# Token halves of 512 and 448 instead of 502 and 500 in a chain of attention and two feed-forward layers

## The chip, the cores and the metric

The kernel runs on one core of a Trainium2 chip. The metric is device time in microseconds (us) of one execution, given as the median of several runs. The engines are TensorE (PE in the profile, with PEld for its weight loads), VectorE (DVE), ScalarE (ACT), GpSimd (POOL) and SyncE (SP, which here issues every DMA).

## What is computed

The reference, cut to what matters (6016 tokens, 256 channels, 2048 hidden units, all float32):

```python
qn = q / (np.linalg.norm(q, axis=1, keepdims=True) + 1e-06)
kn = k / (np.linalg.norm(k, axis=1, keepdims=True) + 1e-06)
s = kn.transpose(0, 2, 1) @ qn / tau          # 256 x 256, channels by channels
a = softmax(s, axis=-1)
x = (v @ a).reshape(6016, 256)
h = x @ moe_w_in                               # 256 -> 2048
x = (h * np.clip(h + 3.0, 0.0, 6.0) / 6.0) @ moe_w_out
h = x @ moe2_w_in
out = np.maximum(h, 0.0) ** 2 @ moe2_w_out
```

## The kernel before, in words

**Start.** Scores are summed over 47 blocks of 128 tokens (`score`, L293, plain float32 matmuls of 256 columns) while q and k stream in, the squares of q and k are summed on ACT and DVE (`squares`, L288), and the 256 x 256 softmax follows. The softmax matrix is multiplied into the first layer's weights (the `m1_*` functions, L440 to L489, matmuls of 512 columns), so that v needs no product of its own.

**Pieces.** The tokens are cut into six pieces, and each piece into two halves of equal width (`WIDTHS`, L24: four pieces of halves of 502 tokens, two of 500; `WMAX` = 502 is the row length of nearly every tile). Tokens lie along the free axis, so a half's width is the number of columns of a matmul. Layer j (0 or 1) treats pieces p = 0 to 5 one after the other, so the kernel works through twelve pairs (j, p).

**High and low parts.** Every float32 operand x is kept as hi (x rounded to float32r, made by a copy on ACT) and lo (x minus hi, made by a subtraction on DVE or POOL); `split`, L115. `passes` (L298) makes one product of three matmuls: L304 multiplies the weights' hi with the tokens' hi, L305 the weights' lo with the tokens' hi, L306 the weights' hi with the tokens' lo. So L306 is the one that streams a lo row. Tokens' hi and lo are the two rows of one tile `[P, 2, WMAX]` (`operand` L495, `g_tile` L578): the lo row begins WMAX numbers behind the hi row.

**The first pair, (0, 0),** is done plainly: 32 steps (`first`, `product`, `second`, L596 to L618) of 12 matmuls each, 384 in all, while the first layer's weights are still being converted.

**The other eleven pairs** go through `strassen` (L702): 8 units to a pair, a unit being a 2 x 2 block product of 7 products in place of 8 (`mult`, targets `x`, `y`, `q`) and 8 products with the second weights (`group`, L551, target `acc`). That makes 15 products, 45 matmuls, to a unit and 360 to a pair. A unit also has 3 copies out of PSUM on ACT (L726), 3 additions on DVE (L730), the activation (L736, L738 on ACT; L744, L749 on DVE), and a hi copy and a lo subtraction for each of four blocks (L753 on ACT, L120 on DVE).

**Order.** It is written by hand: `at(place, ...)` (L643) puts a step at a place, `run` plays the steps in the order of their places, 15 places to a unit. `prepare` (L651) loads the next pair's tokens three and a half units ahead and makes its operands on POOL and ACT (L670 to L685). `second_in` and `second_out` (L212, L249) convert the second layer's weights on ACT, DVE and POOL in the time of pairs (0, 1) to (0, 4). Each pair's result is copied out of PSUM (`evict`, L560) and stored to DRAM, at last to `out`.

**Small tiles.** `ident` and `ones` (L104, L106) lie in the pool `const`. `small(n)` (L270) hands out pieces of four `scratch` tiles of 2 x WMAX numbers, the first tile with room taken first.

Of the kernel before, what the change touches and what calls it, by code (L numbers as in the profile page):

```python
# [8 lines left out]
F32 = mybir.dt.float32  # L9
# [7 lines left out]
P = 128  # L17
# [3 lines left out]
NT = NTOK // P  # L21
KC = C // P
KF = DFF // P
WIDTHS = [502] * 4 + [500] * 2  # L24
NP = len(WIDTHS)
WMAX = max(WIDTHS)
NU = KF // 2
# [23 lines left out]
def attention_then_two_ffns(  # L51
# [32 lines left out]
    const = ctx.enter_context(tc.tile_pool(name="const", bufs=1))  # L84
# [3 lines left out]
    ops = ctx.enter_context(tc.tile_pool(name="ops", bufs=1))  # L88
# [12 lines left out]
        return ps_h.tile(shape, F32, tag=tag, name=name, bufs=2 if tag == "y" else 1)  # L101


    ident = const.tile([P, P], F32, name="ident")  # L104
    make_identity(nc, ident)
    ones = const.tile([P, P], F32, name="ones")  # L106
    nc.gpsimd.memset(ones, 1.0)
    three = const.tile([P, 1], F32, name="three")
    nc.gpsimd.memset(three, 3.0)
# [198 lines left out]
    with tc.manual_schedule():  # L308
# [50 lines left out]
        def load_x(j, p, raw):  # L359

            w = WIDTHS[p]
            for k in range(KC):
# [132 lines left out]
        def operand(j, p, r):  # L495
# [6 lines left out]
            else:  # L502
                t = ops.tile([P, 2, WMAX], F32R, tag=f"op{r}", name=f"x{j}_{p}_{r}")
            t = t[:, :, :WIDTHS[p]]
            operands[j, p, r] = [t[:, i, :] for i in range(2)]
# [5 lines left out]
        def split_first(k):  # L511
            w = WIDTHS[0]
            for n in range(2):
                hi, lo = x0[k, n] = operand(0, 0, ((B11, T3), (B21, B22))[k][n])
                split(hi, lo, raw0[k][:, n, :w])
# [35 lines left out]
        def group(j, p, u, f, n, d, gs, first, last):  # L551

            w = WIDTHS[p]
            if first:
# [355 lines left out]
```

## Time and profile before

| what | value |
|---|---|
| median of 3 runs | 1092.11 us (1091.79 to 1092.32) |
| profiled execution, its own time | 1092.65 us |
| its span, first to last instruction | 1090.9 us |
| PE busy | 1068.3 us, 98% |
| DVE busy | 864.4 us, 79% |
| ACT busy | 675.0 us, 62% |
| POOL busy | 246.3 us, 23% |
| mean granted TensorE clock | 0.993 |

The span starts with the first instruction, and all places in the trace are counted from there. Matmuls overlap: a matmul's recorded length runs from its entering the array to its last result, so the pace of TensorE is read from the distance between the starts of two matmuls, not from their lengths.

### The profile page before, as it was taken

The numbers are of one execution on the slowest core, as the hardware profiler recorded it, in microseconds if no ns is written. First come the engines' busy times: TensorE is split into PE (matmuls) and PEld (weight loads), VectorE is DVE, ScalarE is ACT, GpSimd is POOL, SyncE is SP. The second block draws the span as 40 slices with busy tenths as digits, with TensorE's granted clock in tenths as the row PEclk, the third lists the DMA queues.
The fourth block names the chain that finished last, engine by engine and source line by source line (L and its number), as shares of the span: only waits on it lengthen the run. The fifth ranks groups of instructions, "written<-read, shape, count | busy, mean of one in ns | idle before, by whom it ended". The sixth has DMA issues, their size and how long they took to land.

```text
span 1090.9 us, 13113 instructions
## 1 busy us (share of the span) xinstructions
PE 1068.3 (98%) x4630; PEld 873.8 (80%) x4630; DVE 864.4 (79%) x1283; ACT 675.0 (62%) x1196; POOL 246.3 (23%) x215
## 2 busy tenths in 40 slices
PE   9989899999999999999999999999999999999998
PEld 7868677878878877788888888888888888888886
DVE  6798977888888888888678778778778778778765
ACT  6677667778677767777666455445445445445443
POOL 0022351162342154043013003003003003003000
PEclk9999999999999999999999999999999999999999
DMA  9721302213312311410254100100100100100001
GB/s 348 297 63 34 96 1 78 91 56 113 129 53 77 130 53 51 156 54 28 116 192 175 65 1 29 48 1 29 48 1 23 54 1 10 67 0 16 23 1 38
DMA packets 26451, 77.66 MB, mean 71 GB/s; under 512 B 2833, under 2 KB 11025, under 8 KB 26385
## 3 DMA queue, kind: packets, MB, share of 16 engines
q1 hardware_dynamic: 26384, 76.82, 19.5%
q8 instruction: 36, 0.59, 0.2%
q14 instruction: 31, 0.25, 0.1%
HBM read 52.95 MB, written 23.86 MB: 70 GB/s over the span
## 4 chain that ended last, share of the span: by engine, by line
PE 79%; DVE 10%; issue 4%; ACT 4%; POOL 2%; DMA 1%; SPq 0%; DVEq 0%; POOLq 0%; ACTq 0%
PE acc L306 13%; PE acc L304 13%; PE acc L305 13%; PE y L304 7%; PE y L306 6%; PE y L305 6%; PE q L304 3%; PE s L294 3%; PE q L306 3%; PE q L305 3%; DVE gs L120 3%; DVE g L744 2%; DVE h L730 2%; PE x L304 2%; PE x L306 2%
## 5 line engine op out<-in xcount | busy, mean ns | idle before, releaser
L120 DVE TENSOR_TENSOR gs<-g,gs 128x502 fp32r<-128x502 f32 (+1 forms) x384 | 282.9, 755 | 64.9 <-ACT gs L753 58.9
L306 PE MATMUL acc<-gs,wo 128*128 128x502 f32 (+1 forms) x768 | 302.5, 394 | 0.5 <-DVE gs L120 0.5
L305 PE MATMUL acc<-gs,wo 128*128 128x502 f32 (+1 forms) x768 | 300.7, 392 | 1.1 <-DVE wo L120 1.1
L304 PE MATMUL acc<-gs,wo 128*128 128x502 f32 (+1 forms) x768 | 301.5, 393 | 0.1
L753 ACT CAST gs<-g 128x502 fp32r<-128x502 f32 (+1 forms) x352 | 214.7, 612 | 107.6 <-DVE g L749 54.4
L306 PEld LDWEIGHTS acc<-gs,wo 128*128 128x128 f32 x768 | 146.1, 190 | 32.7 <-DVE gs L120 2.5
L304 PEld LDWEIGHTS acc<-gs,wo 128*128 128x128 f32 x768 | 146.7, 191 | 31.0 <-ACT gs L118 0.8
L305 PEld LDWEIGHTS acc<-gs,wo 128*128 128x128 f32 x768 | 145.7, 190 | 31.5 <-DVE wo L120 1.4
L685 POOL TENSOR_TENSOR x<-raw,x 128x502 fp32r<-128x502 f32 (+1 forms) x55 | 72.8, 1331 | 333.0 <-ACT x L681 332.8
L749 DVE SCALAR_TENSOR_TENSOR g<-h 128x502 f32<-128x502 f32 (+1 forms) x144 | 120.4, 836 | 3.1
L744 DVE SCALAR_TENSOR_TENSOR g<-r,h 128x502 f32<-128x502 f32 (+1 forms) x120 | 97.4, 812 | 29.1 <-ACT r L736 25.2
L736 ACT ACTIVATE r<-h,three 128x502 f32<-128x502 f32 (+1 forms) x120 | 85.9, 716 | 32.5 <-DVE h L730 32.2
L730 DVE TENSOR_TENSOR h<-q,su 128x502 f32<-128x502 f32 (+1 forms) x88 | 59.6, 678 | 48.9 <-PE q L306 48.2
L730 DVE TENSOR_TENSOR h<-q,se 128x502 f32<-128x502 f32 (+1 forms) x88 | 59.7, 678 | 35.9 <-ACT se L726 35.6
L738 ACT ACTIVATE r<-y 128x502 f32<-128x502 f32 (+1 forms) x48 | 28.3, 590 | 88.4 <-PE y L306 88.4
L726 ACT COPY se<-y 128x502 f32<-128x502 f32 (+1 forms) x88 | 50.7, 576 | 41.6 <-PE y L306 41.0
L726 ACT COPY su<-y 128x502 f32<-128x502 f32 (+1 forms) x88 | 50.1, 569 | 34.9 <-PE y L306 34.9
L726 ACT COPY sa<-y 128x502 f32<-128x502 f32 (+1 forms) x88 | 50.2, 571 | 33.5 <-PE y L306 33.1
L730 DVE TENSOR_TENSOR h<-x,sa 128x502 f32<-128x502 f32 (+1 forms) x88 | 59.5, 676 | 10.5 <-PE x L306 9.8
L294 PE MATMUL s<-qk 128*128 128x256 f32 x188 | 43.3, 391 | 0.8 <-DMA qk<-in_qk 0.8
L294 PEld LDWEIGHTS s<-qk 128*128 128x128 f32 x188 | 36.6, 197 | 6.6 <-DMA qk<-in_qk 1.6
L670 POOL TENSOR_TENSOR t<-raw 128x502 f32<-128x502 f32 (+1 forms) x11 | 14.6, 1328 | 112.6 <-DMA raw<-x2d 112.6
(240 smaller groups left out, 1883.9 us busy)
## 6 DMA issues: line engine op xcount, KB each, us to landing
qk<-in_qk SPq DMA_DIRECT2D x23, 512.0 KB, 7.4
wo<-in_w_out SPq DMA_DIRECT2D x16, 512.0 KB, 4.4
wi<-in_w_in SPq DMA_DIRECT2D x10, 512.0 KB, 4.2
wo2d<-wo2s SPq DMA_DIRECT2D x8, 512.0 KB, 3.0
wo<-wo2d SPq DMA_DIRECT2D x8, 512.0 KB, 3.5
x2d<-o SPq DMA_DIRECT2D x16, 251.0 KB, 2.3
raw<-x2d SPq DMA_DIRECT2D x8, 502.0 KB, 4.8
out<-o SPq DMA_DIRECT2D x16, 251.0 KB, 2.3
```

The lines of the kernel that those rows point to most:

```text
L120: (rest or nc.vector).tensor_tensor(out=lo, in0=x, in1=f32(hi), op=ALU.subtract)
L294: nc.tensor.matmul(s_ps[i], lhsT=x[:, C + i * P:C + (i + 1) * P], rhs=x[:, :C], start=(t == 0), stop=(t == NT - 1))
L304: nc.tensor.matmul(ps, lhsT=ah, rhs=bh, start=first, stop=False, skip_group_check=more)
L305: nc.tensor.matmul(ps, lhsT=al, rhs=bh, start=False, stop=False, skip_group_check=more)
L306: nc.tensor.matmul(ps, lhsT=ah, rhs=bl, start=False, stop=last, skip_group_check=more)
L685: nc.gpsimd.tensor_tensor(out=l, in0=ts[r], in1=f32(h), op=ALU.subtract)
L726: nc.scalar.copy(s[tag], s["y"])
L730: nc.vector.tensor_tensor(out=s[which], in0=s[ps], in1=s[tag], op=ALU.add)
L736: nc.scalar.activation(s["r" + which], h, AF.Relu, bias=three)
L744: nc.vector.scalar_tensor_tensor(out=g, in0=s["r" + which], scalar=6.0, in1=h, op0=ALU.min, op1=ALU.mult)
L749: nc.vector.scalar_tensor_tensor(out=g, in0=h, scalar=0.0, in1=r, op0=ALU.max, op1=ALU.mult)
L753: nc.scalar.copy(gs[which][0], s["g" + which])
```

## The change

Only widths, row lengths and the places of a few small tiles change.

```diff
-WIDTHS = [502] * 4 + [500] * 2
+WIDTHS = [512] * 5 + [448]
...
-    ident = const.tile([P, P], F32, name="ident")
+    both = ops.tile([P, 512], F32, tag="t0", name="both")
+    ident, ones = both[:, :P], both[:, P:2 * P]
     make_identity(nc, ident)
-    ones = const.tile([P, P], F32, name="ones")
     nc.gpsimd.memset(ones, 1.0)
```

`WMAX` follows and becomes 512, so every operand tile is `[P, 2, 512]`: the lo row begins 512 numbers behind the hi row, where it began 502 behind. The halves add up to 3008 tokens in either case. `both` takes a buffer (`t0`) that `prepare` uses later for the sums of the tokens' blocks; that frees the room of `ident` and `ones` in the pool `const`. The scratch tiles grow from 1004 to 1024 numbers, and so `small` packs its pieces otherwise: both sums of squares now lie in the first tile, and the fourth stays empty.

On every engine the same instructions stand in the same order as before, and all but one wait are for the same count of the same engine. The one is on ACT, at the copies of the first product's results (`m`, L472, and the first activation, L607): a wait for POOL stands three instructions earlier (`mp` are that product's PSUM tiles, `rs` the softmax's row sums, L464 the hi copies of the new weights). Before:

```order
L464 ACTIVATE a_0_533<-mp_0_501,rs_495 128x256 [waits DVE_49]
L464 ACTIVATE wa_0h<-mp_1_538,rs_509 128x2x256 [waits PE_49]
L472 ACTIVATE m_0_0_547<-mp_0_501,rs_495 128x512 [waits DVE_49]
L472 ACTIVATE m_0_1_549<-mp_1_538,rs_509 128x512 [waits DVE_49]
L152 ACTIVATE tywo_0_529<-wo_0_431 128x512
L607 ACTIVATE r_0_0_579<-h_0_0_565,three 128x502 [waits PE_49,Pool_49]
```

And with the change:

```order
L464 ACTIVATE a_0_532<-mp_0_500,rs_494 128x256 [waits DVE_49]
L464 ACTIVATE wa_0h<-mp_1_537,rs_508 128x2x256 [waits PE_49]
L472 ACTIVATE m_0_0_546<-mp_0_500,rs_494 128x512 [waits DVE_49,Pool_49]
L472 ACTIVATE m_0_1_548<-mp_1_537,rs_508 128x512 [waits DVE_49]
L152 ACTIVATE tywo_0_528<-wo_0_430 128x512
L607 ACTIVATE r_0_0_578<-h_0_0_564,three 128x512 [waits PE_49]
```

What moved is the wait for POOL alone; the width of the activation shows the new half.

## Rows read from the trace of the kernel before

**Rows 1.** The page: busy time of each engine, and the span in 40 slices.

```profile
PE 1068.3 (98%) x4630; PEld 873.8 (80%) x4630; DVE 864.4 (79%) x1283; ACT 675.0 (62%) x1196; POOL 246.3 (23%) x215
...
PE   9989899999999999999999999999999999999998
...
POOL 0022351162342154043013003003003003003000
```

**Rows 2.** Windows by pair: busy us (count) of each engine, granted clock, DMA share, GB/s.

```profile
165.00:249.00 84.00, 81.83 (x349) 64.95 (x349) 68.43 (x102) 63.22 (x113) 27.45 (x27) 1.00 0.22 79
249.00:337.00 88.00, 85.40 (x363) 69.23 (x363) 74.66 (x111) 65.63 (x119) 29.01 (x28) 0.98 0.25 89
337.00:423.00 86.00, 83.03 (x361) 67.40 (x360) 73.39 (x108) 64.63 (x117) 30.28 (x28) 1.00 0.24 86
423.00:507.00 84.00, 83.19 (x364) 67.71 (x363) 70.45 (x106) 63.99 (x116) 29.39 (x28) 1.00 0.22 78
507.00:588.00 81.00, 80.99 (x358) 67.01 (x357) 60.60 (x90) 55.80 (x97) 13.93 (x11) 1.00 0.35 133
...
753.00:835.00 82.00, 82.00 (x361) 67.84 (x360) 63.46 (x91) 40.88 (x73) 14.97 (x11) 1.00 0.07 26
```

**Rows 3.** Timeline of PE: first matmuls of the last pairs' first units (start, length).

```profile
670.68 0.39 PE L304 MATMUL y<-x,wa_0h 128*128 128x502 f32 x1
...
752.92 0.39 PE L304 MATMUL y<-x,wa_0h 128*128 128x502 f32 x1
...
835.22 0.39 PE L304 MATMUL y<-x,wa_0h 128*128 128x502 f32 x1
...
917.58 0.39 PE L304 MATMUL y<-x,wa_0h 128*128 128x500 f32 x1
...
999.39 0.40 PE L304 MATMUL y<-x,wa_0h 128*128 128x500 f32 x1
...
1060.63 0.40 PE L304 MATMUL y<-x,wa_3h 128*128 128x500 f32 x1
```

**Rows 4.** Timeline of PE: matmuls of 512 columns, and the short ones after them.

```profile
54.05 0.39 PE L306 MATMUL mp<-wi1l,eth 128*128 128x512 f32 x1
...
54.97 0.83 PE L280 MATMUL busy<-ones 128*128 128x128 f32 x6
...
106.00 0.40 PE L304 MATMUL mp<-wi1h,eth 128*128 128x512 f32 x1
...
106.93 0.40 PE L305 MATMUL mp<-wi1h,etl 128*128 128x512 f32 x1
```

**Rows 5.** Timeline around the stall at 317 us: PE, ACT.

```profile
317.20 0.39 PE L306 MATMUL acc<-gs,wo 128*128 128x502 f32 x1
...
317.64 0.62 ACT L235 CAST wa2s<-w 128x512 fp32r<-128x512 f32 x1 [1.45 <-POOL w L210]
...
319.90 0.49 PE L304 MATMUL y<-x,wa_3h 128*128 128x502 f32 x1 [2.31 <-ACT su L726]
...
321.51 0.62 PE L304 MATMUL acc<-gs,wo 128*128 128x502 f32 x1
...
321.93 0.62 PE L305 MATMUL acc<-gs,wo 128*128 128x502 f32 x1
```

**Rows 6.** Lines by form (busy us, mean ns): POOL's lo, and DVE additions from PSUM.

```profile
L685 POOL TENSOR_TENSOR x<-raw,x 128x502 fp32r<-128x502 f32 x35 | 46.0, 1322 | 212.1 <-ACT x L681 212.0
...
L730 DVE TENSOR_TENSOR h<-q,se 128x502 f32<-128x502 f32 x56 | 38.0, 678 | 20.2 <-ACT se L726 19.9
...
L291 DVE TENSOR_TENSOR scratch<-sq,scratch 128x512 f32<-128x512 f32 x47 | 29.3, 686 | 7.9 <-ACT sq L290 7.9
```

**Rows 7.** Timeline of the end: the last matmul and the last copy.

```profile
1086.74 0.38 PE L306 MATMUL acc<-gs,wo 128*128 128x500 f32 x1
1087.16 0.57 ACT L570 COPY o<-acc 128x500 f32<-128x500 f32 x1 [1.46 <-PE acc L306]
```

## The prediction

> **What bounds the kernel now.** I read the page first, then the busy time pair by pair, then the pace of the matmuls, then the stalls and the end. On the page PE is busy in nearly every slice [rows 1]. By pairs there are two kinds of stretch. From about 425 us on, nothing holds PE up: a pair of 502 takes 82 us, all of it PE's, while DVE has 18 us to spare [rows 2]. In pairs (0, 1) to (0, 4), and in the plain pair before them, PE idles now and then, because ACT or DVE hands over late: in the window from 337 us PE is busy 83.03 of 86 us [rows 2]. So for two thirds of the time the metric is a count of matmuls times their distance, and that distance is what the change touches.
>
> The distance is read from the first matmuls of successive pairs, 360 matmuls apart [rows 3]. Pair (1, 1): 752.92 - 670.68 = 82.24 us, over 360 = 228.4 ns. Pair (1, 2): 835.22 - 752.92 = 82.30 us, 228.6 ns. So 502 columns take 228.5 ns. Pair (1, 4) with 500 columns: 999.39 - 917.58 = 81.81 us, 227.3 ns; six units of pair (1, 5): 1060.63 - 999.39 = 61.24 us over 270 = 226.8 ns. So 500 columns take 227.0 ns. At the full 2.4 GHz a column is 0.417 ns, so 502 columns are 209.2 ns and 500 are 208.3 ns. What is left on top is **19.3 ns at 502 and 18.7 ns at 500**. Two columns should make 0.83 ns, but 1.5 ns are seen. The cost on top is not the array's own: after the stall at 317 us the clock is at 1.2 GHz, and starts at 321.51 and 321.93 are 0.42 us apart [rows 5], which is 502 columns (418 ns) and nothing more.
>
> **The change, part by part.** Order and waits are the same, so the sum is one of widths.
>
> 1. *Columns.* The plain pair has 384 matmuls, the other eleven 360 each. Before: 384 x 502 + 7 x 360 x 502 + 4 x 360 x 500. After: 384 x 512 + 9 x 360 x 512 + 2 x 360 x 448. The difference is +240 columns (the plain pair grows, and it does more matmuls to a token), 0.1 us. Columns alone decide nothing.
>
> 2. *What stands on top of the columns.* There are 384 + 11 x 360 = 4,344 matmuls of these kinds before and after. My reading of the 0.67 ns between 502 and 500 is that a row costs extra where it does not fill whole groups of four numbers (16 bytes). 502 is not a multiple of four, so all three matmuls of a product have a broken group. 500 is, but its lo row starts 502 numbers in, so one of three has one. Then 0.67 = (1 - 1/3) e, e = 1.0 ns, and a whole row has 19.3 - 1.0 = 18.3 ns on top. With the change all rows are whole: 512 columns cost 213.3 + 18.3 = 231.6 ns, 448 cost 186.7 + 18.3 = 205.0 ns. The row that speaks nearest is that of the 512-column matmuls of the first product, whose rows are whole already: four of them in 54.97 - 54.05 = 0.92 us, four in 106.93 - 106.00 = 0.93 us, 230.0 and 232.5 ns, mean 231.3 [rows 4]. It allows 18.3 ns and, just, 19.
>
>    By pairs, against 228.5 and 227.0: the plain pair +3.1 x 384 = +1.2 us; seven pairs 502 to 512, +3.1 x 360 = +1.1 us each, +7.8; two pairs 500 to 512, +4.6 x 360 = +1.7 each, +3.3; two pairs 500 to 448, -22.0 x 360 = -7.9 each, -15.8. Sum **-3.5 us**. If the cost on top were 18.7 ns for the new rows (no less than now at 500), each of the 4,344 matmuls would cost 0.4 ns more, +1.7 us: -1.8 us. If it were 19.3 ns, +4.3 us: +0.8 us. These are the bounds of this term, -3.5 to +0.8.
>
>    The Trainium skill, SBUF — State Buffer, in its specifications and its box on cachelines, says that SBUF is read in 16-byte lines and that each step to a new line has a price. By it 502 numbers are 125.5 lines, read as 126, worth 504 columns; three rows of 500 average 501.3. Then 2.67 columns, 1.11 ns, should lie between them, against the 1.5 ns of the trace; the estimate from that page is -3.1 us where the rows give -3.5. No row of this trace shows a lo row that starts on a whole line behind its hi row.
>
> 3. *DVE, ACT and POOL.* A DVE operation grows from 678 ns at 502 to 686 ns at 512 [rows 6], 0.8 ns a number. A unit has some eleven on DVE: +0.09 us, while PE's unit grows by 45 x 3.1 = 0.14 us. Conversions of weights stay as they are. So the late engines gain at most 0.05 to 0.1 us a unit on PE, in 32 units up to 2 or 3 us, and only where a stall is theirs. But stalls are also matters of a few hundred ns: the one at 317 us begins with ACT waiting 1.45 us for POOL, becomes 2.31 us on PE, and is followed by matmuls at half clock at 0.42 us [rows 5], each 0.19 us too long. One such train more or less is about 1.5 us. Bounds -2 to +2 us; I take 0, since both signs have a row and neither a size. In the pairs of 448, PE's unit falls to 45 x 205 = 9.2 us. DVE had 60.6 of 81 us in (0, 5) [rows 2], 7.6 us a unit, so it stays below.
>
> 4. *The end.* After the last matmul come one copy of 0.57 us [rows 7] and a store; 448 in place of 500 takes off some 0.06 us. -0.1 us at most; I take -0.1.
>
> 5. *Small tiles.* `both` in `t0` is next written by POOL pairs later. ACT's earlier wait is for POOL's sixth instruction, one of the start's, some 50 us before ACT comes to it; at nothing, since POOL is nearly idle in the first two slices [rows 1]. If that cover were gone, it would be about one POOL operation, 1.3 us [rows 6], within the bounds of term 3. The sums of squares now share a tile, with the same waits as before.
>
> Sum: -3.5 - 0.1 = -3.6 us against the profiled execution's 1092.65 us, which stands 0.5 us over the median 1092.11. A median of **1088.5 us**.
>
> **The rivals.**
>
> *Columns only.* The 0.67 ns is not a matter of broken groups but of the pairs themselves, and new rows carry 18.7 to 19.3 ns. For it: the 232.5 ns at 106 us [rows 4] is 213.3 + 19.2, in rows that are whole. Against it: the other four came at 230.0. Time: -1.8 to +0.8 us, about 1091.6 us.
>
> *A floor under 448.* Each matmul has a weight load of 128 columns beside it; if its path cannot go below some distance, the 720 matmuls of 448 columns do not reach 205.0 ns. With a floor x ns above that the change is -3.6 + 0.72 x us: it loses from x = 5, and by more than 0.2% (2.2 us, about what a measurement of this kernel tells from no change) from x = 8. At a floor of 217 ns the time is 1088.5 + 8.6 = 1097.1 us; with none of the fall below 227.0 it would be 1104.3. Against it: six matmuls of 128 columns, each with its own load, take 0.83 us in all [rows 4], under 140 ns each. For it: those are plain float32, and no float32r matmul below 500 columns is in the trace.
>
> *The whole cost on top goes.* Were the 18 ns a matter of rows that start off a line, the change could take most of it away. The Trainium skill, TensorE: Matmul & The Clock Gate, under the back-to-back issue gap, gives columns over 2.4 plus 2.5 ns. By the trace, 512-column rows that are whole already pay 231 ns, not 216 [rows 4]. From the rows, 4,344 matmuls less 16 ns would be -70 us, 1022 us. I give it 0.02.
>
> *Stalls.* Shorter trains in (0, 1) to (0, 4) on top of the forecast, down to -6 us, 1086; chance 0.08.
>
> **How the numbers follow.** Forecast (whole rows cheaper) 0.46, columns only 0.34, floor 0.10, stalls 0.08, whole cost 0.02. With the 2 us either way of term 3: the forecast gives faster by over 0.2% three times in four (0.35); columns only gives it in one of seven (0.05); stalls and whole cost always (0.10): 0.50. Slower by over 0.2%: 0.07 of the floor, 0.05 of columns only: 0.12. Within: 0.38. The range runs from 1085.5 (forecast less 3) to 1094.0 (columns only at +0.8 plus 1.5); it leaves out most of the floor, the whole cost, half of stalls, and the edges, together two in ten.
>
> **What would show it.** In the changed kernel's trace the first matmuls of successive pairs from 671 us on should be 83.4 us apart at 512 (231.6 ns) and the last pair's at 73.8 us (205.0 ns); 83.7 and 74.2 would be columns only. A last pair of 78 us would be the floor. If those distances hold and the total does not, look at the idle time of PE between 50 and 450 us, which I took as unchanged: that is where the forecast is weakest.

## The result, and the profile after

The changed kernel takes **1079.37 us** (median of 4 runs, 1079.04 to 1079.98) against 1092.21 us before: a ratio of 0.9883, with a 95% interval of 0.9866 to 0.9900. The forecast was 1088.5 us; the gain is 12.8 us where 3.6 were forecast, and the time lies below the range. The profiled execution has a span of 1077.8 us, 13.1 us less than before.

The page after, beside [rows 1]: PE is busy 18.9 us less, DVE 2.2 us more.

```profile
PE 1049.4 (97%) x4630; PEld 865.8 (80%) x4630; DVE 866.6 (80%) x1283; ACT 672.5 (62%) x1196; POOL 256.5 (24%) x215
```

The timeline of PE after, first matmuls of the last pair of layer 0, of pairs of layer 1 and of some of their units (start, length), beside [rows 3]:

```profile
511.94 0.36 PE L304 MATMUL y<-x,wa_0h 128*128 128x448 f32 x1
...
586.21 0.39 PE L304 MATMUL y<-x,wa_0h 128*128 128x512 f32 x1
...
667.62 0.39 PE L304 MATMUL y<-x,wa_0h 128*128 128x512 f32 x1
...
688.02 0.39 PE L304 MATMUL y<-x,wa_1h 128*128 128x512 f32 x1
...
728.82 0.39 PE L304 MATMUL y<-x,wa_3h 128*128 128x512 f32 x1
...
749.52 0.39 PE L304 MATMUL y<-x,wa_0h 128*128 128x512 f32 x1
...
1013.76 0.36 PE L304 MATMUL y<-x,wa_1h 128*128 128x448 f32 x1
...
1050.24 0.36 PE L304 MATMUL y<-x,wa_3h 128*128 128x448 f32 x1
```

From the third unit to the seventh of pair (1, 1), 180 matmuls of 512 columns take 728.82 - 688.02 = 40.80 us: **226.7 ns** each, where 231.6 were forecast and 502 columns took 228.5. Ten columns more cost less than before. The whole pair takes 749.52 - 667.62 = 81.90 us; 0.3 us go to short waits in its last units. In the same stretch of the trace every start comes 226 or 227 ns after the last one; before, the distances varied between 220 and 238 ns. In the last pair 180 matmuls of 448 columns take 1050.24 - 1013.76 = 36.48 us: **202.7 ns**, where 205.0 were forecast.

For the place of the gain the same timeline of the kernel before is wanted at two more points:

```profile
506.52 0.40 PE L304 MATMUL y<-x,wa_0h 128*128 128x500 f32 x1
...
588.43 0.40 PE L304 MATMUL y<-x,wa_0h 128*128 128x502 f32 x1
```

| stretch | before, us | after, us | measured | forecast |
|---|---|---|---|---|
| to the start of pair (0, 5) | 506.5 | 511.9 | +5.4 | +6.2 |
| pair (0, 5) | 81.9 | 74.3 | -7.6 | -7.9 |
| layer 1, to the end of the span | 502.5 | 491.6 | -10.9 | -1.9 |

The forecast column is the prediction's own terms by pair: +1.2, three times +1.1, +1.7; then -7.9; then four times +1.1, +1.7, -7.9 and the end. So layer 0 came out close to the forecast, and nearly all of the miss is in layer 1, where hardly anything but the distance of matmuls counts. Each place is read from one profiled execution; in a second one of the changed kernel (the last run below) pair (0, 5) begins at 510.37 us, 1.6 us earlier, so a difference of 1 or 2 us in the early stretch tells little.

That layer 0 fits is partly chance. Matmuls settle there at 226.7 ns too, but PE waits longer. The waits of PE between 165 and 510 us, the kernel before (who waits for whom: us in total, times, longest):

```profile
PE y L304 <- ACT su L726: 4.2, 5, 2.3
PE q L304 <- DVE h L730: 2.1, 2, 1.8
PE y L304 <- ACT se L726: 1.1, 3, 0.7
PE y L304 <- ACT sa L726: 1.0, 2, 0.6
```

and the changed kernel:

```profile
PE y L304 <- ACT su L726: 5.4, 7, 2.6
PE y L304 <- ACT se L726: 2.5, 3, 0.9
PE q L304 <- DVE h L730: 2.2, 2, 1.9
PE y L304 <- ACT sa L726: 1.3, 3, 0.8
```

They grow from 8.4 to 11.4 us. A wider count takes every matmul whose successor starts over 100 ns later than its columns need at 2.4 GHz, and adds up that excess less 20 ns each; stretches at half clock are in it. By it the loss goes from 15.3 to 21.2 us, and to 19.4 us in the second execution of the changed kernel.

### The profile page after: what moved, and what is told of

It reads as the page before. It is cut to its first block, busy times and chain, and to the rows that moved or that the text cites. A ratio compares the mean times of both kernels' runs of the same rounds, so it can differ in the third digit from the quotient of the medians.

```text
span 1077.8 us, 13113 instructions
## 1 busy us (share of the span) xinstructions
PE 1049.4 (97%) x4630; PEld 865.8 (80%) x4630; DVE 866.6 (80%) x1283; ACT 672.5 (62%) x1196; POOL 256.5 (24%) x215
## 4 chain that ended last, share of the span: by engine, by line
PE 75%; DVE 12%; ACT 6%; issue 5%; POOL 2%; DMA 1%; SPq 0%; DVEq 0%; ACTq 0%; POOLq 0%
PE acc L304 13%; PE acc L306 13%; PE acc L305 13%; PE y L304 7%; PE y L306 6%; PE y L305 6%; PE q L304 3%; PE s L294 3%; PE q L306 3%; PE q L305 3%; DVE gs L120 3%; DVE g L744 3%; DVE h L730 2%; PE x L304 2%; PE x L306 2%
## 5 line engine op out<-in xcount | busy, mean ns | idle before, releaser
L120 DVE TENSOR_TENSOR gs<-g,gs 128x512 fp32r<-128x512 f32 (+1 forms) x384 | 280.5, 748 | 65.1 <-ACT gs L753 58.8
L305 PE MATMUL acc<-gs,wo 128*128 128x512 f32 (+1 forms) x768 | 297.0, 387 | 1.1 <-DVE wo L120 1.1
L306 PE MATMUL acc<-gs,wo 128*128 128x512 f32 (+1 forms) x768 | 297.3, 387 | 0.7 <-DVE gs L120 0.7
L304 PE MATMUL acc<-gs,wo 128*128 128x512 f32 (+1 forms) x768 | 297.4, 387 | 0.1
L753 ACT CAST gs<-g 128x512 fp32r<-128x512 f32 (+1 forms) x352 | 214.3, 611 | 116.0 <-DVE g L749 59.3
L306 PEld LDWEIGHTS acc<-gs,wo 128*128 128x128 f32 x768 | 144.7, 188 | 30.6 <-DVE gs L120 3.3
L305 PEld LDWEIGHTS acc<-gs,wo 128*128 128x128 f32 x768 | 144.8, 189 | 28.7 <-DVE wo L120 1.4
L304 PEld LDWEIGHTS acc<-gs,wo 128*128 128x128 f32 x768 | 144.9, 189 | 28.4 <-ACT gs L118 0.8
L685 POOL TENSOR_TENSOR x<-raw,x 128x512 fp32r<-128x512 f32 (+1 forms) x55 | 78.1, 1428 | 324.9 <-ACT x L681 323.7
L749 DVE SCALAR_TENSOR_TENSOR g<-h 128x512 f32<-128x512 f32 (+1 forms) x144 | 123.8, 860 | 3.1
L744 DVE SCALAR_TENSOR_TENSOR g<-r,h 128x512 f32<-128x512 f32 (+1 forms) x120 | 99.8, 832 | 28.7 <-ACT r L736 24.9
L736 ACT ACTIVATE r<-h,three 128x512 f32<-128x512 f32 (+1 forms) x120 | 85.6, 713 | 33.5 <-DVE h L730 32.8
L730 DVE TENSOR_TENSOR h<-q,su 128x512 f32<-128x512 f32 (+1 forms) x88 | 59.6, 677 | 40.2 <-PE q L306 40.0
L730 DVE TENSOR_TENSOR h<-q,se 128x512 f32<-128x512 f32 (+1 forms) x88 | 59.5, 676 | 33.0 <-ACT se L726 32.9
L730 DVE TENSOR_TENSOR h<-x,sa 128x512 f32<-128x512 f32 (+1 forms) x88 | 59.4, 675 | 8.4 <-PE x L306 7.3
```

Source lines behind the costliest of these rows:

```text
L120: (rest or nc.vector).tensor_tensor(out=lo, in0=x, in1=f32(hi), op=ALU.subtract)
L304: nc.tensor.matmul(ps, lhsT=ah, rhs=bh, start=first, stop=False, skip_group_check=more)
L305: nc.tensor.matmul(ps, lhsT=al, rhs=bh, start=False, stop=False, skip_group_check=more)
L306: nc.tensor.matmul(ps, lhsT=ah, rhs=bl, start=False, stop=last, skip_group_check=more)
L685: nc.gpsimd.tensor_tensor(out=l, in0=ts[r], in1=f32(h), op=ALU.subtract)
L730: nc.vector.tensor_tensor(out=s[which], in0=s[ps], in1=s[tag], op=ALU.add)
```

## The experiments

Distances below are read as above, from the third unit's first matmul to the seventh's, 180 matmuls later. In some kernels a line or two are added ahead, and L304 is then L305 or L306. Edits are cut to the lines that matter, with names shortened.

### The old widths on rows of 512

```diff
-WIDTHS = [512] * 5 + [448]
+WIDTHS = [502] * 4 + [500] * 2
-WMAX = max(WIDTHS)
+WMAX = 512
```

> The changed kernel with the old widths (four pairs of 502, two of 500) but rows of 512 numbers, so only the start of the lo row moves against the kernel before (from 2008 to 2048 bytes behind the hi row). Theory A, the start of the lo row decides: 502 and 500 columns settle at 226.7 ns or less like 512, a pair of 502 in layer 1 takes 81.6 us or less in place of 82.3, and the kernel takes 1084 to 1088 us. Theory B, whole widths decide: 228.5 ns stay, 82.2 to 82.3 us a pair, 1091 to 1093 us.

Measured: 1086.14 us, ratio 0.9933 (0.9914 to 0.9952). The timeline in pair (1, 1):

```profile
690.59 0.39 PE L304 MATMUL y<-x,wa_1h 128*128 128x502 f32 x1
...
730.79 0.39 PE L304 MATMUL y<-x,wa_3h 128*128 128x502 f32 x1
```

40.20 us over 180 is 223.3 ns, and pair (1, 4) with 500 columns has 223.3 as well. So widths as such are not it: spacing the rows at 512 takes 5.2 ns off 502 columns and 3.7 off 500. (More than the start of the lo row moves here, other than the expectation says: with rows of 512 numbers every tile begins elsewhere too. The later runs take that up.) Over half of the gain, 0.67 of 1.17%, comes with the row length alone. And 500 and 502 cost the same, so a broken group of four at the end of a row costs nothing that is seen here. Pair (0, 5) begins at 508.36 us, where it was 506.52 before: with faster matmuls and the same tokens the early stretch gained nothing that can be seen.

### The lo row 8 bytes further on

```diff
-t = ops.tile([P, 2, WMAX], F32R, ...)
+t = ops.tile([P, 2 * WMAX + 2], F32R, ...)
-[t[:, i, :] for i in range(2)]
+[t[:, i * (WMAX + 2):i * (WMAX + 2) + w] for i in range(2)]
```

> The changed kernel (512 and 448) with the lo row 8 bytes further on in each operand tile (514 numbers behind the hi row). Theory A, the start of the lo row decides: the settled 226.7 ns are lost, 512 columns take 231 to 233 ns (83.2 to 83.9 us a pair), 448 columns 205 or more, and the kernel takes 1087 to 1096 us. Theory B, whole widths decide: 226.7 and 202.7 ns stay, and 1079 to 1080 us.

Measured: 1092.36 us, ratio 0.999 (0.9981 to 1.0). In pair (1, 1):

```profile
694.55 0.39 PE L305 MATMUL y<-x,wa_1h 128*128 128x512 f32 x1
...
736.21 0.39 PE L305 MATMUL y<-x,wa_3h 128*128 128x512 f32 x1
```

41.66 us over 180 is 231.4 ns; the even pairs have 232.4, and 448 columns take 203.8 in place of 202.7. Nearly the whole gain is gone. That looked like theory A, the start of the lo row; it was not the whole matter, as the runs from "Which rows" on show, since the longer tiles also moved every tile that follows.

### Six widths

```diff
-WIDTHS = [512] * 5 + [448]
+WIDTHS = [512, 496, 504, 508, 500, 488]
```

> The changed kernel with six widths, 512, 496, 504, 508, 500 and 488, on rows of 512 numbers; what is read is the distance of matmuls in each pair of layer 1. Theory A16, a row costs by the groups of 16 numbers (64 bytes) that it begins: 512, 504, 508 and 500 have 32 groups and all take 226.7 ns, 496 and 488 have 31 and take 219.6. Theory A4, by columns with one fixed cost: 226.7, 220.0, 223.3, 225.0, 221.7 and 216.7 ns. Theory B, whole widths decide: 512 and 496 (multiples of 16) below the line of the others by 1 ns and more.

Measured: 1086.66 us, ratio 0.9936 (0.9917 to 0.9955). The distances are 226.7, 220.0, 226.7, 227.6, 226.7 and 220.0 ns for 512, 496, 504, 508, 500 and 488 columns; for 496 and 500:

```profile
691.22 0.38 PE L304 MATMUL y<-x,wa_1h 128*128 128x496 f32 x1
...
730.82 0.38 PE L304 MATMUL y<-x,wa_3h 128*128 128x496 f32 x1
...
935.12 0.39 PE L304 MATMUL y<-x,wa_1h 128*128 128x500 f32 x1
...
975.91 0.39 PE L304 MATMUL y<-x,wa_3h 128*128 128x500 f32 x1
```

A4 and B are wrong: width is not followed column by column. A16 fits all but 508, yet it does not hold either: the same 500 columns on the same rows took 223.3 ns in the run with the old widths and 226.7 here. Settled distances stand on steps of 3.33 ns, 8 cycles at 2.4 GHz (220.0, 223.3, 226.7; only 508 lies off them), and which step a width below 512 gets is not a matter of the width alone. Even inside this run 488 columns take 220.0 ns in pair (1, 5) and 225.1 in pair (0, 5), where no distance is over 242 ns.

### 448 first

```diff
-WIDTHS = [512] * 5 + [448]
+WIDTHS = [448] + [512] * 5
```

> The changed kernel with the pair of 448 first in place of last. It is the plain pair of layer 0, which does more matmuls to a token, so 1,536 columns fewer are streamed in all, 0.6 us. Theory C, PE's matmuls set the time of the early stretch too: 1078 to 1079.5 us. Theory D, the early stretch is set by conversions on ACT, DVE and POOL, and a plain pair that is 24 ns a matmul (9.2 us) shorter on PE gives less than half of that while the last pair of layer 0 grows by its 7.6 us: 1082 to 1086 us.

Measured: 1084.53 us, ratio 0.9912 (0.9893 to 0.9931); theory D. The last pair of layer 0, now of 512:

```profile
507.73 0.39 PE L304 MATMUL y<-x,wa_0h 128*128 128x512 f32 x1
...
589.85 0.36 PE L304 MATMUL y<-x,wa_0h 128*128 128x448 f32 x1
```

It begins at 507.73 us and not at 511.94, so 64 columns less in 384 matmuls, 9.2 us of PE by the 24 ns between the two paces, bought 4.2 us (2.6 against the second execution of the changed kernel); and the pair takes 82.1 us where 448 took 74.3. So the early stretch is held by more than PE's matmuls, and tokens are cheap there and dear after it. That is the second part of the gain: the change puts 52 more tokens of each half into the early stretch and takes them out of pair (0, 5). Against the run with the old widths, which has the same rows, the early stretch grows by 511.94 - 508.36 = 3.6 us and pair (0, 5) shrinks by 7.1 us (from 81.3 to 74.3). Layer 1 shrinks by another 2.6 us (from 494.2 to 491.6), since 512 columns at 226.7 ns are cheaper to a token than 502 at 223.3. By spans, then, the rows gave 7.0 us (1090.9 to 1083.9) and the widths on such rows 6.1 (to 1077.8).

### Conversions further apart, in the changed kernel and in the one before

```diff
-at0 = (2 + 3.5 * u) * SLOTS // 1
+at0 = (2 + 4.2 * u) * SLOTS // 1
```

> The changed kernel with the second layer's weight conversions 4.2 units apart in place of 3.5, so that they reach into the last pair of layer 0. Theory D, ACT and DVE set the early stretch and PE's gain there went into waits for them: PE's waits between 165 and 510 us, 21 us, fall to half or less, the pairs at 512 come nearer to 81.6 us each, and the kernel takes 1066 to 1074 us. Theory C, the waits there come from something else (loads, the order of PE's own steps): 1078 to 1081 us.

> The kernel before with the same spacing of 4.2 units. Beside the run of the changed kernel with that spacing it tells what the change is worth where conversions hold PE up less. Theory D: PE's waits between 165 and 510 us, 15 us, fall to half, 1083 to 1088 us, and the changed kernel then gains more than 13 us on it, 14 to 19 us. Theory C: 1091 to 1093 us.

Measured: the changed kernel 1076.44 us, ratio 0.9849 (0.9835 to 0.9864); the kernel before 1091.39 us, ratio 0.9981 (0.9972 to 0.9991). The waits of PE between 165 and 510 us in the changed kernel with the wider spacing:

```profile
PE y L304 <- ACT se L726: 4.2, 4, 1.4
PE y L304 <- ACT su L726: 3.1, 6, 0.8
PE y L304 <- ACT sa L726: 2.1, 4, 1.1
PE q L304 <- DVE h L730: 0.6, 3, 0.2
```

Theory D has the right sign and too large a size: in the changed kernel the waits fall from 11.4 to 10.0 us, not to half, and the longest from 2.6 to 1.4 us. In the kernel before they fall from 8.4 to 7.9 us, and its time lies in theory C's range. By the wider count the changed kernel's loss falls from 21.2 to 16.6 us, but some 3 us of the 21.2 are half clock, which the same kernel does not always have. Near 322 us both executions of the changed kernel wait for the same copy (2.57 and 2.55 us); the granted clock falls in the first and not in the second:

```profile
320.00:327.00 7.00, 4.82 (x14) 3.83 (x15) 4.59 (x5) 5.10 (x9) 7.00 (x6) 0.76 0.57 206
320.00:327.00 7.00, 4.70 (x21) 3.90 (x22) 4.50 (x5) 5.14 (x10) 7.00 (x6) 1.00 0.57 206
```

Against the second, at full clock as this run is, the fall is from 19.4 to 16.6 us. The change is worth 15.0 us at this spacing (1091.39 to 1076.44) and 12.8 at the old one. **The changed kernel with conversions 4.2 units apart has the lowest ratio of this study,** 0.3% under the changed kernel's; its interval (to 0.9864) just touches that of the changed kernel's second measurement (0.986 to 0.989).

> The changed kernel with the conversions 4.6 units apart. Theory D, conversions hold PE up in the early stretch: a further 1 to 3 us on the spacing of 4.2 (ratio to the kernel before 0.985), so a ratio of 0.982 to 0.984. If the waits only move behind the early stretch: a ratio of 0.984 to 0.987.

With 4.6 for 4.2: 1082.45 us, ratio 0.9909 (0.989 to 0.9927), worse than both. The windows of 165 to 510 and 510 to 586 us (busy us and count of PE, PEld, DVE, ACT, POOL; clock; DMA) with 4.6:

```profile
165.00:510.00 345.00, 334.32 (x1443) 268.18 (x1441) 289.65 (x415) 258.02 (x454) 115.14 (x102) 1.00 0.21 74
510.00:586.00 76.00, 70.71 (x338) 63.17 (x339) 60.51 (x97) 54.25 (x103) 19.28 (x18) 1.00 0.50 182
```

and with 4.2:

```profile
165.00:510.00 345.00, 334.60 (x1443) 267.79 (x1442) 287.52 (x418) 259.07 (x456) 117.00 (x103) 1.00 0.22 77
510.00:586.00 76.00, 75.10 (x362) 67.56 (x362) 62.57 (x99) 57.03 (x107) 22.90 (x20) 1.00 0.50 174
```

The early stretch gains nothing more, and in the pair of 448 PE now idles 5.3 of 76 us where it was 0.9. DVE and ACT are not busier there than with 4.2. Ahead of the longest of these waits ACT itself stands 3.57 us for a transfer, the input of the next conversion:

```profile
536.70 0.67 ACT L149 ACTIVATE tbwi<-wi 128x512 f32<-128x512 f32 x1 [3.57 <-DMA wi<-in_w_in]
...
540.92 0.47 PE L304 MATMUL y<-x,wa_1h 128*128 128x448 f32 x1 [2.29 <-ACT sa L726]
```

The copy `sa` that PE waits for comes behind that conversion on ACT, and between the two ACT pauses for 0.17 us at most. Neither theory had this.

### Two pairs of 480

```diff
-WIDTHS = [512] * 5 + [448]
+WIDTHS = [512] * 4 + [480] * 2
```

> The changed kernel with four pairs of 512 and two of 480. Theory A, a settled matmul whose width is a multiple of 16 takes its columns and 32 more at 2.4 GHz (544 for 512, 528 for 496): 480 takes 512 columns' time, 213.3 ns, the two narrow pairs of layer 1 take 76.8 us each, layer 1 gains 1 us on the changed kernel, and the total is 1077 to 1080 us. Theory F, below 496 another cost grows, as 448 took 202.7 ns and not 200.0: 480 takes 215 to 217 ns and the total is 1080 to 1083 us.

Measured: 1082.72 us, ratio 0.9909 (0.9895 to 0.9924). In the last pair:

```profile
1015.60 0.38 PE L304 MATMUL y<-x,wa_1h 128*128 128x480 f32 x1
...
1054.60 0.38 PE L304 MATMUL y<-x,wa_3h 128*128 128x480 f32 x1
```

39.00 us over 180 is 216.7 ns, one step of 3.33 above 213.3: theory F's size. Of the widths tried, 512 is the cheapest to a column (0.4427 ns; 480 has 0.4514, 448 has 0.4524).

### Where the lo rows start

```diff
+OFFS = [0, 4, 8, 2, 16, 12]
-WIDTHS = [512] * 5 + [448]
+WIDTHS = [504] * 4 + [496] * 2
-[t[:, i, :] for i in range(2)]
+[t[:, i * (512 + OFFS[p]):i * (512 + OFFS[p]) + w] for i in range(2)]
```

> The changed kernel with widths 504 (four pairs) and 496 (two), and the lo row of the pairs 0 to 5 starting 0, 16, 32, 8, 64 and 48 bytes further on than 2048 behind the hi row; what is read is the distance of matmuls in each pair of layer 1. Without an offset 504 takes 226.7 ns and 496 takes 220.0. Theory A64, the lo row must start on a multiple of 64 bytes: 226.7, then 229 to 232 for 16, 32 and 8 bytes, 220.0 for 64, 223 or more for 48. Theory A16, a multiple of 16 bytes is enough: only the pair with 8 bytes is dearer than 226.7. Theory A32: the pairs with 16, 8 and 48 bytes are dearer, that with 32 is not.

Measured, one run: 1093.3 us; distances of 226.7 ns (0), 226.7 (16 bytes), 225.6 (32), 231.1 (8), 224.4 (64) and 224.4 (48).

At 504 this reads like A16. At 496 it does not: a lo row moved by a whole 64 bytes stands 4.4 ns above the 220.0 that 496 had with none. But that was another pair of another run; in this same pair (1, 4), with no row moved, a later run has 223.3. So the two pairs of 496 settle nothing.

### Which rows

Each pair of the changed kernel gets its own starts of rows, in tiles of 1028 numbers:

```diff
+ROWS = [((0, 514), (0, 512)), ((0, 512), (0, 514)), ((0, 514), (0, 514)),
+        ((2, 516), (2, 516)), ((0, 512), (0, 512)), ((0, 514), (0, 512))]
```

> The changed kernel (512 and 448) where each pair has its own starts of rows in the operand tiles, read again as distances of matmuls in layer 1: pair 0 has only the lo rows of the tokens' operands 8 bytes off a multiple of 16 (7 of 15 products), pair 1 only those of the activations (8 of 15), pair 2 both, pair 3 the hi rows 8 bytes off and the lo rows on a multiple of 16, pair 4 none, pair 5 (448) as pair 0. Theory G, each matmul that streams a row 8 bytes off pays for itself: pair 2 takes 231.5 to 232.5 ns, pairs 0 and 1 stand about half way (229 to 230), pair 3, with two such rows in three, takes 236 to 239, pair 4 takes 226.7. Theory H, the beat between PE and its loads is lost as soon as any row is off: pairs 0 to 3 all take 231 to 233 ns.

Measured, one run: 1093.37 us; 232.6, 232.2, 232.4 and 233.1 ns in pairs 0 to 3, and in pair 4, where no row was moved:

```profile
945.46 0.39 PE L306 MATMUL y<-x,wa_1h 128*128 128x512 f32 x1
...
987.23 0.39 PE L306 MATMUL y<-x,wa_3h 128*128 128x512 f32 x1
```

41.77 us over 180, 232.1 ns. That control is the finding, and neither theory expected it. Its lo row is 2048 bytes behind its hi row, and every row starts on a multiple of 32 bytes. What is new is that the longer tiles no longer start at one address modulo 2048 bytes. In the changed kernel all streamed rows do, by the addresses of the built program; in the kernel before the rows of layer 1 started at 24 different ones.

### All rows together, and tiles 64 bytes longer

```diff
-WIDTHS = [512] * 5 + [448]
+WIDTHS = [504] * 4 + [496] * 2
+OFFS_X, OFFS_G = [0, 2, 0, 8, 0, 16], [0, 2, 8, 8, 0, 16]
-[t[:, i, :] for i in range(2)]
+[t[:, i + OFF[p]:i + OFF[p] + w] for i in (0, 512)]
```

> The changed kernel with widths 504 (four pairs) and 496 (two), where the start of all streamed rows of a pair is moved together: pair 0 by 0, pair 1 by 8 bytes, pair 3 by 32, pair 4 by 0, pair 5 by 64; in pair 2 the activations' rows (hi and lo) start 32 bytes further on than the tokens' operands. Read as distances of matmuls in layer 1. Theory E, what counts is that all streamed rows start at the same address modulo 2048 bytes, wherever that is: pairs 0, 1 and 3 are alike (226.7 ns or less), pairs 4 and 5 are alike (220 ns), and pair 2 may be dearer. Theory A, each row must start on a multiple of 16 bytes by itself: pair 1, where every row is 8 bytes off, takes 231 ns or more, above the other pairs of 504.

```diff
-t = ops.tile([P, 2, WMAX], F32R, tag=f"op{r}", ...)
+t = ops.tile([P, 2 * WMAX + 16], F32R, tag=f"op{r}", ...)
```

> The changed kernel (512 and 448) with each tile of tokens' operands 64 bytes longer, so that its rows still start on multiples of 64 bytes and the lo row 2048 bytes behind the hi row, but no longer at the same address modulo 2048 from tile to tile (odd pairs keep two of seven operands elsewhere, at the old spacing). Theory E, the same start modulo 2048 counts: the 226.7 ns are lost, 228 to 232.5 ns at 512 columns. Theory A, a start on a multiple of 64 (or 16) bytes is enough: 226.7 ns in every pair of 512, and 1078 to 1080 us.

Measured, one run each: 1091.44 and 1091.5 us beside 1093.27 of the kernel before. The second, in pair (1, 1):

```profile
693.53 0.40 PE L304 MATMUL y<-x,wa_1h 128*128 128x512 f32 x1
...
735.16 0.40 PE L304 MATMUL y<-x,wa_3h 128*128 128x512 f32 x1
```

41.63 us over 180, **231.3 ns**, 231.6 in the other pairs, though every row starts on a multiple of 64 bytes and every lo row 2048 bytes behind its hi row. That is against A at 512 columns, and what E expects: **a start on whole lines is not enough, and 226.7 ns at 512 columns were seen only where all streamed rows start at one address modulo 2048 bytes.** Without it, the rows of 512 cost 231.3, and the kernel gains 0.2% in its one run. Two things are not shown. Starts alike modulo 64 do not do, but no modulus between 64 and 2048 was tried. And the longer tiles pushed the pool of ACT's and DVE's intermediate tiles 512 bytes on as well; no run at 512 columns moves the streamed rows alone.

The first run shows that a row's own start counts too, a little. Pairs (1, 1) and (1, 3), all rows 8 and 32 bytes on:

```profile
691.83 0.39 PE L306 MATMUL y<-x,wa_1h 128*128 128x504 f32 x1
...
733.23 0.39 PE L306 MATMUL y<-x,wa_3h 128*128 128x504 f32 x1
...
856.47 0.39 PE L306 MATMUL y<-x,wa_1h 128*128 128x504 f32 x1
...
897.27 0.39 PE L306 MATMUL y<-x,wa_3h 128*128 128x504 f32 x1
```

41.40 us (230.0 ns, each distance the same) and 40.80 us (226.7 ns, as in pair 0). So 8 bytes off costs one step of 3.33 ns even where all rows start alike. Pair 2, with two starts 32 bytes apart, has 228.7, and that is a mean of two kinds. The three matmuls of a product on tokens' operands, whose rows start just where they do in pair 0, take mostly 228, 234 and 233 ns (231.1 on the mean); those on the activations, whose rows were moved, stay at 226.6:

```profile
775.68 0.39 PE L306 MATMUL x<-x,wa_1h 128*128 128x504 f32 x1
...
776.38 0.39 PE L306 MATMUL acc<-gs,wo 128*128 128x504 f32 x1
...
777.06 0.39 PE L306 MATMUL y<-x,wa_1h 128*128 128x504 f32 x1
```

So a row can become dearer because others moved, and no theory of single rows says that. Theory E has its own misses below 512 columns. In the run on lo rows, at 504 columns, hi and lo rows started 16 and 32 bytes apart at no price (226.7 and 225.6 ns). At 496 columns pair 4 here has 223.3 and pair 5 226.7, both with all rows alike, where 496 had 220.0 among the six widths. What sets the step of widths below 512 **stays open**.

### The changed kernel once more

No edit; beside the runs with 4.6 units.

> The changed kernel once more, on the chip of the two runs beside it and with the same runs of the kernel before: a ratio of 0.987 to 0.990, PE at 226.7 ns in pairs of 512. Both theories expect the same.

Measured: 1078.67 us, ratio 0.9875 (0.986 to 0.989), and 226.7 ns in all five pairs of 512 of layer 1.

## Why the prediction was wrong

**What bounds the kernel: right.** From 425 us on the time is the number of matmuls times their distance, and the gain is where that says: 10.9 of 13.1 us in layer 1.

**Columns: right.** +240 columns decide nothing.

**What stands on top of the columns: the step that failed, in its size and its cause.** The prediction took e = 1.0 ns for a broken group of four numbers from the difference between 502 and 500, and so 18.3 ns on top of the columns of whole rows. Measured are 226.7 - 213.3 = 13.3 ns at 512 and 202.7 - 186.7 = 16.0 at 448. On 4.9 ns too much at 512 hang 5 x 360 matmuls of layer 1, 8.8 us, and 2.3 ns at 448 make another 0.8: 9.6 us, for the 9.0 us that layer 1 missed (the short waits at the ends of pairs take some of it back). The cause was another as well. On rows of 512 numbers, 502 and 500 columns cost the same 223.3 ns, so a broken group at the end of a row cost nothing. Both widths carried the price of the old layout, in which rows started at 24 addresses modulo 2048 and half of them 8 bytes off a line of 16, and the difference between them could not show it. How that price shares out between unlike starts and starts off a line was not measured at 502; at 512, the layout with unlike starts, all on whole lines, costs 4.6 ns (231.3 against 226.7). Why unlike starts cost anything is open.

**The row that should have warned** was taken for support. The 512-column matmuls of [rows 4], at 230.0 and 232.5 ns, were whole rows and seemed to bound the new distance from below. The four at 54.05 run right behind a wait. In the changed kernel, whose settled distance is 226.7, the same four behind the same wait still take 0.93 us, 232.5 ns each: a price of matmuls that have not settled. The four at 106.00 follow no wait: the matmul ahead of them in the kernel before starts 0.23 us earlier, at 105.77, and PE does not wait in the 6 us ahead of it. What they carried was the old layout. In the changed kernel the first three of them, from 103.46 to 103.91, start 226 and 227 ns apart, until a wait of PE's cuts the group. The line of the kernel before, and those of the changed kernel:

```profile
105.77 0.39 PE L306 MATMUL h<-x,wa_1h 128*128 128x502 f32 x1
```

```profile
53.01 0.39 PE L306 MATMUL mp<-wi1l,eth 128*128 128x512 f32 x1
...
53.94 0.83 PE L280 MATMUL busy<-both 128*128 128x128 f32 x6
...
103.46 0.39 PE L304 MATMUL mp<-wi1h,eth 128*128 128x512 f32 x1
...
103.91 0.39 PE L306 MATMUL mp<-wi1l,eth 128*128 128x512 f32 x1
105.71 0.50 PE L304 MATMUL mp<-wi1h,eth 128*128 128x512 f32 x1 [1.41 <-ACT wi1h L118]
```

A row of the kernel before prices the kernel before, whole or not: neither half of [rows 4] was the new settled distance.

**The page on lines.** Rows that start 8 bytes off a line of 16 do cost more (230.0 against 226.7 ns at 504 columns, all else alike). The Trainium skill, SBUF — State Buffer, in its box on cachelines, agrees in sign. The estimate worked out from it, -3.1 us, had the change wrong by four times: in the run with tiles 64 bytes longer all rows start on whole lines, and the distance is 231.3 ns.

**DVE, ACT and POOL, taken at 0 within 2 us: too small.** The loss between 165 and 510 us grew by 5.9 us (4.1 in the second execution), past the bound; it swallowed what PE gained there, and so the early stretch came out near the forecast for the wrong reason. The term priced the growth by DVE's additions (678 to 686 ns; they take 687 to 689 at 512); POOL's subtraction of [rows 6] went from 1322 to 1446 ns, and what that was worth no run tells. The other half of that term, that these engines keep up with 448 columns, held.

**The end and the small tiles: right,** as far as they can be seen; the last copy takes 0.53 us for 0.57.

**The rivals.** No floor under 448: 202.7 ns. Columns only: the total misses it by 12 us, although it is close to what the run with tiles 64 bytes longer shows, 0.2% of gain. The whole cost on top did not go, but 6 of its 19 ns did at 512, which the prediction gave 0.02 in its extreme form and nothing in between. The gap that the Trainium skill, TensorE: Matmul & The Clock Gate, gives under the back-to-back issue gap for an isolated matmul (columns over 2.4 plus 2.5 ns, 215.8 ns for 512) was the settled distance of 512 columns in none of these runs. The upper end of the range, columns only at +0.8 plus 1.5, adds up to 1094.4 and not 1094.0, which decides nothing here.

## What to carry to other kernels

Where matmuls stream float32r rows without a pause, try one spacing of 2048 bytes for all streamed tiles, so that every row starts at the same address modulo 2048, and full rows of 512: here that was 226.7 ns in place of 231.3 to 233.1. Take the price of a matmul from a settled stretch and not from a few behind a wait, do not price a fault from two rows that both have it, and do not take a row of the old layout as a bound for the new one. A pace that improves everywhere pays only where PE is the bound: before adding up, mark the stretches where it waits, and move width (or other work) to where it costs least.

## What the runs showed of the hardware

- With all streamed rows starting alike, most mean distances in layer 1 stand on steps of 3.33 ns, 8 cycles at 2.4 GHz: 216.7, 220.0, 223.3, 226.7 and 230.0 ns were seen. Some are even, matmul by matmul: 512 at 226.7 (226 or 227 every time in the run of the result), 488 and 496 at 220.0 among the six widths, 504 at 230.0 with all rows 8 bytes off. Others are even only in the mean: 480 goes between 212 and 221 ns, 502 on rows of 512 between 219 and 230. Two lie off the steps: 448 (202.7, between 199 and 207) and 508 (227.6).
- The same width on the same rows can settle on different steps: 500 columns at 223.3 or 226.7 ns, 496 at 220.0 or 223.3 (226.7 with all rows 64 bytes on). What picks the step was not found.
- Behind a wait the first distance of matmuls of 512 columns is about 335 ns; then come four to ten between 224 and 240 ns, 232 on the mean, before the 226.7 come back (changed kernel).
- The same wait of PE (2.57 and 2.55 us, near 322 us) was followed by half the clock in one execution of the changed kernel (0.76 in the window of 320 to 327 us) and by the full clock in the other.
